# Two accumulating banks in the first channel layer, and nine of twelve second-layer rounds as block products

## The chip, the cores and the metric

The kernel runs on one core of a Trainium2 chip. The metric is the device time of one execution in microseconds (us), the median of several runs; lower is better. The engines are TensorE (PE in the profile; PEld is its weight load), VectorE (DVE), ScalarE (ACT), GpSimd (POOL) and SyncE (SP), which only issues DMAs. All arithmetic that matters here is fp32, and each fp32 matmul in the code shows as two MATMUL instructions in the trace.

## The reference

Attention with a block mask, then a Fourier mixing block with a two-layer channel network:

```python
batch, n_heads, seq, head_dim = (4, 8, 768, 64)
scores = np.where(mask, scale * q @ k.T, -1e9)      # mask: neighbours, first/last and sampled blocks
attn = softmax(scores); x = attn @ v                # bridged to (4, 768, 512)
mixed = np.real(np.fft.fft(np.fft.fft(x, axis=1), axis=2))
u = x + mixed
un = (u - mean(u)) / np.sqrt(var(u) + 1e-06)
ch = np.maximum(un @ w_ch1, 0.0) @ w_ch2            # 512 -> 2048 -> 512
return u + ch
```

## The kernel before, in words

Python code lays out one static instruction stream for each engine, in program order (`manual_schedule`). A small planner keeps a clock for each engine (`when`, advanced by `busy(engine, us, after)`), and decides by it what is issued where.

*Attention* goes in 96 slots (`slot`), 24 a batch. A slot makes two score tiles (L578) in the two PSUM banks of the pool `ps_s`, exponentiates them on ScalarE (in batches 2 and 3 in place, L606), multiplies them by the mask on VectorE (L608), adds the results up on POOL (L638), and multiplies by the values two slots later (L652). Once channel work exists, slots go in pairs: the even one of a pair does all value products that are due, the odd one may do channel work after its scores.

*Mixing* of a batch (`fourier`) is a list of steps, `apart`, that `gap()` inserts between other work where the planner's clocks allow: scaling and folds on VectorE (kind "d"), then products along the sequence (`along`, L856) and across the channels (`across`, L887 to L904), whitening (L951), transposes (`un_flip`, L992, with a copy L993), and operand sums (`right`, L1029). The steps from the first transpose on may start only when at most six entries of channel work are left.

*Channel work* of batches 0 to 2 is the list `late`: four rounds of eight entries, two quads of the first layer and six plain steps of the second. `quad(p)` (L1054) makes two 128-row blocks of the hidden layer for all 768 tokens as two halves, with seven block products in place of eight (the Strassen-Winograd scheme). Its seven products (L1075, 128x384, two matmuls each) are: one into the middle bank `xp`, copied by ScalarE (L1095); one into the middle bank `yp`, used twice; and four into the score banks `z5` and `z7`, each started anew. VectorE adds them up in seven sums (L1080), and ScalarE applies the ReLU in place (L1084). VectorE also forms the operand sums of the next quad (`combine`, `left`, L1042 to L1049). The second layer of a round, `channels` (L1230), is six plain steps of four 512-wide matmuls (L1240) and one VectorE sum (L1243), or, where `seven[r]` is set, three calls of `round_of` (L1171): for a block of tokens in each half seven block products of two 256-wide matmuls (L1183), ScalarE copies (L1188), VectorE sums (L1192, L1222, L1168), and POOL sums (L1152, L1165, L1196). `seven[r]` is set at L1062, only for work done alone, and not for a batch's last round.

How much channel work goes between the attention slots is set at L1606 to L1616: a pace a slot from the planned time left less `COVER`, and `rest()` (L1488), which lets a step go when half of its planned time is owed. The rest is done alone by `until` (L1462) at slot 4 of the next batch but one, when the room of the old batch is needed; the next batch's mixing steps are inserted there. The last batch is done alone at the end, with its own version of the second layer (`outputs`), and is not touched by the change but for its first layer.

Of the kernel before, what the change touches and what calls it, by code (L numbers as in the profile page):

```python
# [99 lines left out]
def kernel(  # L100
# [460 lines left out]
    def scores(us):  # L561

        n, w = divmod(us[0], UP)
# [409 lines left out]
    z_at = [0.0, 0.0]  # L973
    rstd_at = deque()
# [3 lines left out]
    def mixer(b, xA, xB):  # L978
# [75 lines left out]
        def quad(p):  # L1054
# [5 lines left out]
            if not last:  # L1060
                if p % 2 == 0:
                    seven[p // 2] = state["alone"] and p // 2 < NF // 4 - 1  # L1062
                elif seven[p // 2]:
                    state["drain"]()
                    sums_room()
                    for j in (1, 2, 4, 3):
                        round_right(p // 2, j)
# [5 lines left out]
            def product(to, a, c, after=0.0):  # L1073
                for k in range(ND // 2):
                    nc.tensor.matmul(to, a[:, k, :], c[:, k, :], start=(k == 0),  # L1075
                                     stop=(k == ND // 2 - 1))
                return busy("PE", PRODUCT, after) + HOP

            def plus(to, ps, a, at):
                tt(out=to, in0=ps, in1=a, op=ALU.add)  # L1080
                return busy("DVE", SUM, at) + HOP

            def relu(h, at):
                nc.scalar.activation(out=h, in_=h, func=ACT.Relu)  # L1084
                busy("ACT", RELU, at)

            def combine(j):
# [3 lines left out]
            x, at = ps_m.tile([P, 512], FP32, tag="m", name="xp")[:, 0:HS], bank("m")  # L1091
            z5, z7 = (ps_s.tile([P, 2, 512], FP32, tag="s", name=name)[:, 0, 0:HS]
                      for name in ("z5", "z7"))
            done = product(x, a11, b11)
            nc.scalar.copy(out=h11, in_=x)  # L1095
            p1 = busy("ACT", RELU, done) + HOP
            give(at, p1 - HOP)
            y, at = ps_m.tile([P, 512], FP32, tag="m", name="yp")[:, 0:HS], bank("m")
            p2 = product(y, a12, b21)
            done = product(z7, s2, t[2])  # L1100
            u2 = plus(h21, z7, h11, max(done, p1))
            c11 = plus(h11, y, h11, p2)
            relu(h11, c11)
            done = product(z5, s[1], t[1])
            plus(h12, z5, h21, done)
            combine(1)
            done = product(z7, s[3], t[3], u2)
            u3 = plus(h21, z7, h21, done)
            c22 = plus(h22, z5, h21, done)
            z_at[0] = c22  # L1110
            relu(h22, c22)
            combine(3)
            gap(0.0, 1.9)
            done = product(y, a22, t[4], c11)
            c21 = plus(h21, y, h21, done)
            give(at, c21 - HOP)
            relu(h21, c21)
            gap(0.0, 1.9, "t")
            done = product(z7, s[4], b22, u3)
            z_at[1] = plus(h12, z7, h12, done)  # L1120
            relu(h12, z_at[1])
# [10 lines left out]
        def sums_room():  # L1132

            def cut(t, at, k):
                return t[:, at:at + 2 * HS // 3 * k].rearrange("p (k n) -> p k n", k=k)

            rooms = [ep.tile([P, 2 * HS], FP32, tag="e", name="of") for _ in range(4)]
# [7 lines left out]

        def part(r, k, n):
            return w2_sb[:, 4 * r + 2 * k:4 * r + 2 * k + 2, n * DH:n * DH + DH]

        def round_right(r, j):
            a, c = {1: (part(r, 0, 1), part(r, 0, 0)), 2: (part(r, 1, 1), w_t[1]),  # L1150
                    3: (part(r, 1, 1), part(r, 0, 1)), 4: (part(r, 1, 0), w_t[2])}[j]
            nc.gpsimd.tensor_tensor(out=w_t[j], in0=a, in1=c, op=ALU.subtract)  # L1152
            busy("POOL", 1.35)
# [5 lines left out]
        def round_left(m, j):  # L1159
# [4 lines left out]
            if j > 2:  # L1164
                nc.gpsimd.tensor_tensor(out=to, in0=a, in1=c, op=op)  # L1165
                busy("POOL", 0.75, when["DVE"])
            else:
                tt(out=to, in0=a, in1=c, op=op)  # L1168
                busy("DVE", 0.43)

        def round_of(r, m):  # L1171

            after = dict(zip(OUT, OUT[1:])).get(m)
# [4 lines left out]
            u_at, d_at = (ps_s.tile([P, 2, 512], FP32, tag="s", name=name)[:, 0, 0:DH]  # L1178
                          for name in ("yz", "yw"))
# [15 lines left out]
            def later(to, i, at):  # L1195
                nc.gpsimd.tensor_add(out=to, in0=kept[i], in1=to)  # L1196
                busy("POOL", 0.75, at)

            def ahead(*js):
                if after is not None:  # L1200
                    for j in js:
                        round_left(after, j)

            if m == OUT[0]:
                round_left(m, 1)
                round_left(m, 2)
# [3 lines left out]
            k0 = keep(0, u_at, product(u_at, a11, part(r, 0, 0), True, z_at[0]))  # L1210
# [3 lines left out]
            if m == OUT[0]:  # L1214
                round_left(m, 3)
                round_left(m, 4)
            gap(start=0.9)
            k1 = keep(1, u_at, product(u_at, a21, w_t[2], False, k0))
            later(a1, 1, k1)
            k2 = keep(2, d_at, product(d_at, h_s[1], w_t[1], True, z_at[1]))  # L1220
# [3 lines left out]
            z_at[0] = busy("DVE", 0.7, done) + HOP  # L1224
            later(b1, 2, max(z_at[0], k2))
            z_at[1] = plus(a1, d_at, product(d_at, h_s[4], part(r, 1, 1), False, k2))
            ahead(1, 2, 3, 4)
            state["soon"] = 1.6

        def channels(r, half, m):  # L1230

            if seven.get(r):
                round_of(r, m)
                if m == OUT[-1]:
                    for _ in range(T):
                        late.popleft()
                return
# [56 lines left out]
        def outputs(r, m, after):  # L1294
# [27 lines left out]
            ends = r == 1 and after is None  # L1322
            u = sum_p.tile([P, DH], FP32, tag="oT", name="u")
# [457 lines left out]
```

## Time and profile before

| what | value |
|---|---|
| median of three runs | 1064.43 us (1063.6 to 1065.32) |
| the profiled execution, own time | 1066.03 us |
| its span, first to last instruction | 1064.3 us |
| mean granted TensorE clock | 0.987 |
| PE / VectorE / ScalarE / POOL busy | 1026.7 / 708.7 / 382.5 / 328.3 us |
| L1075, first-layer products, PE busy in all | 297.6 us |
| L1240, plain second-layer steps, PE busy in all | 148.8 us |
| L1183, second-layer block products, PE busy in all | 93.4 us |

Lines of a group show: line, engine, operation, output and input tiles, shapes, count, then busy time, mean ns of one, idle time before them and what ended it. Timeline rows show: start, duration, engine, line, operation, tiles, count, and in brackets the idle time before, with what released the engine. Rows of windows show, after the stretch and its width, busy time and count of PE, PEld, DVE, ACT and POOL, then the granted clock, the DMA share and GB/s. Neighbouring matmuls overlap a little in the trace, so a group's sum is best taken from starts.

### The profile page before, as it was taken

How to read it: one execution, taken by the hardware profiler on the slowest of the kernel's cores; microseconds unless marked ns; L12 is line 12 of the kernel's file. 1: busy time of each engine (PE TensorE's matmuls, PEld its weight loads, DVE VectorE, ACT ScalarE, POOL GpSimd, SP SyncE). 2: the span in 40 equal slices, each digit the busy share in tenths (PEclk: the TensorE clock that was granted, in tenths of full speed). 3: DMA queues.
4: the chain of work that ended last, by engine and by line, in shares of the span. 5: the costliest groups of instructions: out<-in, count | busy, mean ns of one | idle time of the engine just before them, and what ended most of it. 6: DMA issues, size and time to landing. Idle time of an engine off the chain costs nothing.

```text
span 1064.3 us, 13217 instructions
## 1 busy us (share of the span) xinstructions
PE 1026.7 (96%) x4594; PEld 572.3 (54%) x4594; DVE 708.7 (67%) x1287; ACT 382.5 (36%) x781; POOL 328.3 (31%) x365
## 2 busy tenths in 40 slices
PE   8999999999999998899999999799999999999996
PEld 4333345445766853444444764353445764578575
DVE  6898795877776566754668476765447736675663
ACT  6978765563222214342430223333221221210210
POOL 1000183556733404545561222645440401000000
PEclk9999999999999999999999999999999999899998
DMA  7857422220000002212120001311000002000001
GB/s 211 229 170 225 107 46 45 45 46 15 1 1 1 1 20 69 38 38 32 35 54 0 1 1 39 67 28 24 8 15 1 1 1 57 3 1 1 1 17 47
DMA packets 120549, 46.32 MB, mean 44 GB/s; under 512 B 108172, under 2 KB 113562, under 8 KB 120474
## 3 DMA queue, kind: packets, MB, share of 16 engines
q1 hardware_dynamic: 119222, 44.66, 17.6%
q10 hardware_dynamic: 1220, 0.72, 0.3%
q8 instruction: 38, 0.62, 0.2%
q14 instruction: 37, 0.30, 0.1%
q0 software_dynamic: 32, 0.01, 0.0%
HBM read 36.72 MB, written 6.29 MB: 40 GB/s over the span
## 4 chain that ended last, share of the span: by engine, by line
PE 84%; DVE 5%; ACT 4%; POOL 2%; issue 2%; DMA 1%; SPq 1%; ACTq 0%; DVEq 0%; POOLq 0%
PE z L1075 15%; PE y L1240 13%; PE s L578 12%; PE o L652 10%; PE yp L1075 7%; PE yy L1308 7%; PE xp L1075 4%; PE yz L1183 3%; PE yw L1183 2%; PE yc L1183 2%; PE zp L856 2%; PE s L588 1%; POOL acc L638 1%; ACT e L598 1%; PE sp L719 1%
## 5 line engine op out<-in xcount | busy, mean ns | idle before, releaser
L638 POOL TENSOR_TENSOR acc<-acc,e 128x384 f32<-128x384 f32 x158 | 162.6, 1062 | 97.0 <-DVE e L608 77.9
L578 PE MATMUL s<-qT,kT 64*128 64x384 f32 x768 | 155.3, 519 | 7.6 <-ACT e L598 5.2
L652 PE MATMUL o<-e,vr 128*64 128x384 f32 x768 | 146.1, 508 | 5.0 <-DVE oT L660 5.0
L638 POOL TENSOR_TENSOR acc<-e 128x384 f32<-128x384 f32 x46 | 49.0, 1084 | 202.4 <-ACT e L598 126.0
L578 PEld LDWEIGHTS s<-qT,kT 64*128 64x128 f32 x768 | 64.7, 188 | 86.5 <-ACT e L598 23.1
L608 DVE TENSOR_TENSOR e<-s,mask 128x768 f32<-128x768 f32 x88 | 79.9, 948 | 46.2 <-ACT s L606 35.6
L606 ACT ACTIVATE s<-s 128x768 f32<-128x768 f32 x88 | 66.8, 791 | 106.1 <-PE s L578 105.7
L598 ACT ACTIVATE e<-s 128x768 f32<-128x768 f32 x104 | 79.0, 809 | 49.0 <-PE s L588 36.5
L1075 PE MATMUL z<-unT,t 128*128 128x384 f32 x256 | 93.4, 488 | 1.6 <-DVE hA L1080 1.6
L652 PEld LDWEIGHTS o<-e,vr 128*64 128x64 f32 x768 | 48.5, 139 | 77.0 <-issue 67.5
L1080 DVE TENSOR_TENSOR hA<-z,hA 128x384 f32<-128x384 f32 x64 | 35.6, 557 | 70.0 <-PE z L1075 70.0
L1084 ACT ACTIVATE hA<-hA 128x384 f32<-128x384 f32 x64 | 33.5, 523 | 123.7 <-DVE hA L1080 123.7
L1240 PE MATMUL y<-w_sb,hA 128*128 128x512 f32 x168 | 74.8, 595 | 0.0
L1240 PE MATMUL y<-w_sb,hB 128*128 128x512 f32 x168 | 74.5, 595 | 0.0
L1196 POOL TENSOR_TENSOR x<-of,x 128x256 f32<-128x256 f32 x45 | 34.9, 783 | 123.2 <-ACT of L1188 83.4
L1075 PEld LDWEIGHTS z<-unT,t 128*128 128x128 f32 x256 | 48.3, 190 | 36.9 <-DVE hA L1080 4.0
L1243 DVE TENSOR_TENSOR x<-y,x 128x512 f32<-128x512 f32 x42 | 29.0, 691 | 57.3 <-PE y L1240 57.3
L1084 ACT ACTIVATE hB<-hB 128x384 f32<-128x384 f32 x64 | 33.5, 523 | 87.2 <-DVE hB L1080 87.2
L1240 PEld LDWEIGHTS y<-w_sb,hB 128*128 128x128 f32 x168 | 31.2, 190 | 38.2 <-issue 38.2
L1240 PEld LDWEIGHTS y<-w_sb,hA 128*128 128x128 f32 x168 | 31.1, 190 | 37.5 <-issue 36.7
L1075 PE MATMUL xp<-unT,w_sb 128*128 128x384 f32 x128 | 49.0, 506 | 0.0
L1075 PE MATMUL z<-t,w_sb 128*128 128x384 f32 x128 | 46.6, 487 | 0.2 <-DVE e L608 0.2
(235 smaller groups left out, 1728.5 us busy)
## 6 DMA issues: line engine op xcount, KB each, us to landing
wraw<-in_moe_w_ch_dram SPq DMA_DIRECT2D x32, 512.0 KB
vr<-in_v_dram SPq DMA_DIRECT2D x30, 192.0 KB
qb<-in_q_dram SPq DMA_DIRECT2D x44, 96.0 KB
kb<-in_k_dram SPq DMA_DIRECT2D x44, 96.0 KB
x<-oT SPq DMA_DIRECT2D x192, 12.0 KB
out_dram<-x SPq DMA_DIRECT2D x11, 252.0 KB
out_dram<-x SPq DMA_DIRECT2D x18, 128.0 KB
qr<-in_q_dram SPq DMA_DIRECT2D x24, 64.0 KB
```

Source lines behind the costliest of these rows:

```text
L578: nc.tensor.matmul(s[:, i, 0:HS], kT[rows, c * P:(c + 1) * P], qT[rows, queries], start=True, stop=u not in by_pe)
L598: nc.scalar.activation(out=e, in_=s[:, :, 0:HS], func=ACT.Exp, scale=scale)
L606: nc.scalar.activation(out=s[:, :, 0:HS], in_=s[:, :, 0:HS], func=ACT.Exp, scale=scale)
L608: nc.vector.tensor_tensor(out=e, in0=s[:, :, 0:HS], in1=m.broadcast_to([P, 2, HS]), op=ALU.mult)
L638: nc.gpsimd.tensor_add(out=acc[:, i, :], in0=start[:, i, :], in1=e[:, i, :])
L652: nc.tensor.matmul(o[D * i:D * i + D, :], vt[:, i, c, :], e[:, i, :], start=(c == 0), stop=(c == C - 1))
L1075: nc.tensor.matmul(to, a[:, k, :], c[:, k, :], start=(k == 0), stop=(k == ND // 2 - 1))
L1080: tt(out=to, in0=ps, in1=a, op=ALU.add)
L1084: nc.scalar.activation(out=h, in_=h, func=ACT.Relu)
L1183: nc.tensor.matmul(to, a[:, k, :], c[:, k, :], start=start and k == 0, stop=k == 1, skip_group_check=True)
L1240: nc.tensor.matmul(y, hs[0, half][:, l, m * P:(m + 1) * P], w2_sb[:, 4 * r + l, :], start=(l == 0), stop=(l == 3))
L1308: nc.tensor.matmul(ps, a[:, k, :], c[k // 2][:, k % 2, :] if isinstance(c, list) else c[:, k, :], start=(k == 0), stop=(k == 3))
```

## The change

Four things are changed at once.

In `quad`, the first product goes into a score bank (`za`) and not into a middle bank. Later products are accumulated into the same bank (`start` false), and ScalarE copies the bank's content out between them (`keep`), so that of seven VectorE sums three remain. `zb` is the second score bank. The last ReLU reads the bank directly. `two_tiles` names the two banks in the order in which they were emptied. One of the two inner `gap` calls goes, the other gets 1.4 for 1.9.

`choose` decides at a round's first quad how its second layer is done: "e" in work done alone (with rooms of the pool `ep`, as before), "big" between attention slots if no mixing step is pending (with two rooms of `big`, and all operand sums on VectorE), and plain for the last round of a batch. It replaces six plain entries in `late` by three blocks, planned at 6.1 each.

`round_of` takes its two score banks through `two_tiles`, and in a round's first token block starts with a product into a score bank.

`COVER` is 117 for 100, and `rest()` lets nothing go between slots while more than 6 and at most 24 entries are left, that is rounds 1 to 3 of a batch. `begin` first finishes an open "big" round.

```diff
+    def two_tiles(name):
+        pair = [ps_s.tile([P, 2, 512], FP32, tag="s", name=name + str(i))[:, 0, :]
+                for i in range(2)]
+        return state["first"], pair[::-1] if state["first"] else pair
...
                 if p % 2 == 0:
-                    seven[p // 2] = state["alone"] and p // 2 < NF // 4 - 1
+                    choose(p // 2)
                 elif seven[p // 2]:
-                    state["drain"]()
-                    sums_room()
+                    sums_room(seven[p // 2])
...
-            def product(to, a, c, after=0.0):
+            def product(to, a, c, start, after=0.0):
                 for k in range(ND // 2):
-                    nc.tensor.matmul(to, a[:, k, :], c[:, k, :], start=(k == 0),
-                                     stop=(k == ND // 2 - 1))
+                    nc.tensor.matmul(to, a[:, k, :], c[:, k, :], start=start and k == 0,
+                                     stop=k == ND // 2 - 1, skip_group_check=True)
                 return busy("PE", PRODUCT, after) + HOP
...
+            i, pair = two_tiles("z")
+            za, zb = (t[:, 0:HS] for t in pair)
+            state["first"] = 1 - i
+            k1 = keep(h11, za, product(za, a11, b11, True, z_at[i]))
             y, at = ps_m.tile([P, 512], FP32, tag="m", name="yp")[:, 0:HS], bank("m")
-            p2 = product(y, a12, b21)
-            done = product(z7, s2, t[2])
-            u2 = plus(h21, z7, h11, max(done, p1))
-            c11 = plus(h11, y, h11, p2)
+            c11 = plus(h11, y, max(k1, product(y, a12, b21, True)))
+            give(at, c11 - HOP)
+            k2 = keep(h12, za, product(za, s2, t[2], False, k1))
+            k4 = keep(h22, zb, product(zb, s[1], t[1], True, z_at[1 - i]))
             relu(h11, c11)
-            done = product(z5, s[1], t[1])
-            plus(h12, z5, h21, done)
             combine(1)
-            done = product(z7, s[3], t[3], u2)
-            u3 = plus(h21, z7, h21, done)
-            c22 = plus(h22, z5, h21, done)
-            z_at[0] = c22
+            gap(0.0, 1.4)
+            done = product(za, s[3], t[3], False, k2)
+            c22 = plus(h22, za, max(done, k4))
+            z_at[1 - i] = plus(h12, zb, product(zb, s[4], b22, False, k4))
             relu(h22, c22)
             combine(3)
-            gap(0.0, 1.9)
-            done = product(y, a22, t[4], c11)
-            c21 = plus(h21, y, h21, done)
-            give(at, c21 - HOP)
-            relu(h21, c21)
-            gap(0.0, 1.9, "t")
-            done = product(z7, s[4], b22, u3)
-            z_at[1] = plus(h12, z7, h12, done)
-            relu(h12, z_at[1])
+            done = product(za, a22, t[4], False, c22)
+            relu(h12, z_at[1 - i])
+            z_at[i] = relu(h21, done, za)
             combine(4)
...
+        def choose(r):
+
+            seven[r] = None
+            if r < NF // 4 - 1 and late:
+                seven[r] = "e" if state["alone"] else None if apart else "big"
+            if seven[r]:
+                quad_next = late.popleft()
+                for _ in range(2 * T):
+                    late.popleft()
+                late.extendleft((lambda m=m: round_of(r, m), 6.1) for m in OUT[::-1])
+                late.appendleft(quad_next)
+                state["open"] = T + 1 if seven[r] == "big" else 0
...
+        def aside(r, out, a, c, op, n, at=0.0, sooner=False):
+
+            if seven[r] == "big" or sooner:
+                tt(out=out, in0=a, in1=c, op=op)
+                return busy("DVE", n * 0.0011 + 0.15, at) + HOP
+            nc.gpsimd.tensor_tensor(out=out, in0=a, in1=c, op=op)
+            return busy("POOL", n * 0.0026 + 0.07, at) + HOP
...
-            u_at, d_at = (ps_s.tile([P, 2, 512], FP32, tag="s", name=name)[:, 0, 0:DH]
-                          for name in ("yz", "yw"))
+            i, pair = two_tiles("yz")
+            u_at, d_at = (t[:, 0:DH] for t in pair)
...
+            def first():
+                k.append(keep(0, u_at, product(u_at, a11, part(r, 0, 0), True, z_at[i])))
 
             if m == OUT[0]:
-                round_left(m, 1)
-                round_left(m, 2)
+                for j in (1, 2):
+                    round_left(r, m, j)
+                first()
             c_at, at = ps_m.tile([P, 512], FP32, tag="m", name="yc")[:, 0:DH], bank("m")
             a_at = plus(a0, c_at, product(c_at, a12, part(r, 1, 0), True))
             give(at, a_at - HOP)
-            k0 = keep(0, u_at, product(u_at, a11, part(r, 0, 0), True, z_at[0]))
+            if m != OUT[0]:
+                first()
...
-    COVER = 100.0
+    COVER = 117.0
+    KEPT = (NF // 4 - 1) * (2 + 2 * T)
...
     def begin(b):
 
+        while state["open"]:
+            channel_step()
+            gap()
...
     def rest():
 
-        return state["owed"] if late and state["owed"] >= late[0][1] / 2 else 0.0
+        if not late or 2 * T < len(late) <= KEPT or state["owed"] < late[0][1] / 2:
+            return 0.0
+        return state["owed"]
```

## The prediction

> **What bounds the kernel now.** I read the busy table first, then the windows of 25 us, then the timeline of TensorE in three places. The busy table:
>
> ```profile
> PE 1026.7 (96%) x4594; PEld 572.3 (54%) x4594; DVE 708.7 (67%) x1287; ACT 382.5 (36%) x781; POOL 328.3 (31%) x365
> ```
>
> TensorE is the bound: 1064.3 − 1026.7 = 37.6 us of it are idle. So two things count: matmul time, and waits of TensorE. VectorE's 67% counts only where TensorE waits for it. The chain of waits agrees: 84% of the span is PE. The windows say where the idle time lies:
>
> ```profile
> 400.00:425.00 25.00, 22.32 (x93) 10.12 (x93) 16.66 (x24) 10.99 (x20) 12.66 (x16) 0.95 0.31 74
> 425.00:450.00 25.00, 22.20 (x91) 10.24 (x87) 19.39 (x25) 9.56 (x21) 15.16 (x14) 0.91 0.24 37
> 500.00:525.00 25.00, 25.00 (x101) 11.72 (x99) 11.93 (x19) 8.43 (x18) 6.92 (x8) 1.00 0.19 37
> 675.00:700.00 25.00, 21.95 (x96) 10.43 (x97) 18.71 (x23) 10.73 (x22) 15.55 (x15) 0.93 0.24 51
> 900.00:925.00 25.00, 21.97 (x74) 13.36 (x73) 18.17 (x39) 7.09 (x13) 3.31 (x7) 0.86 0.08 21
> ```
>
> The first number after the width is PE busy, the third from the end the granted clock. PE loses time, and clock, three times, where a batch's channel work runs out and the next batch's Fourier mixing isn't ready: I call these the three seams (around 400-440, 650-690, 900-908). Between the seams, as at 500-525, PE is full. The timeline of TensorE, at the seams, in attention, and in the rounds:
>
> ```profile
> 421.16 0.66 PE L992 MATMUL utp<-ident,un 128*128 128x128 f32 x4 [1.94 <-DVE un L951]
> ...
> 436.25 2.83 PE L652 MATMUL o<-e,vr 128*64 128x384 f32 x8 [2.51 <-DVE oT L660]
> ...
> 454.25 1.56 PE L578 MATMUL s<-qT,kT 64*128 64x384 f32 x8
> ...
> 456.11 1.82 DVE L608 TENSOR_TENSOR e<-s,mask 128x768 f32<-128x768 f32 x2 [1.16 <-ACT s L606]
> 456.53 1.56 PE L1075 MATMUL xp<-unT,w_sb 128*128 128x384 f32 x4
> ...
> 459.21 1.45 PE L1075 MATMUL z<-t,w_sb 128*128 128x384 f32 x4
> ...
> 524.57 1.72 PE L578 MATMUL s<-qT,kT 64*128 64x384 f32 x8
> 527.58 1.78 PE L578 MATMUL s<-qT,kT 64*128 64x384 f32 x8 [1.29 <-DVE e L608]
> ...
> 565.26 10.46 PE L1240 MATMUL y<-w_sb,hB 128*128 128x512 f32 x24
> 575.57 1.45 PE L1075 MATMUL xp<-unT,w_sb 128*128 128x384 f32 x4
> ...
> 597.87 1.03 PE L1183 MATMUL yc<-w_sb,hA 128*128 128x256 f32 x4
> 598.73 1.03 PE L1183 MATMUL yz<-w_sb,hA 128*128 128x256 f32 x4
> ```
>
> **A, products of the second layer: −10.3 us.** A plain round starts at 554.86 and the next quad at 575.57: 20.71 us. A block product starts 0.864 us after the one before (597.87, 598.73), and a round has 21: 18.14. Batch 0 already has three such rounds, batches 1 and 2 one each (L1183: 60 matmuls a group, 12 a round, so five). Nine means four more: 4 × 2.57 = 10.3. Their operand sums lie on POOL when channel work is alone (there PE waited for POOL 0.6 us in all five rounds), and on VectorE in the two rounds between attention slots, where VectorE is idle half of the time (11.9 of 25 us at 500-525): nothing. The added ScalarE copies (three of 0.37 a block) go to an engine 36% busy: nothing.
>
> **B, first layer: its first product moves into a score bank: +10.1 us.** Seven products of 1.29 us stay. Four of seven VectorE sums (0.56 each) go, two ScalarE copies (0.48) come. In a quad alone, a copy starts 0.09 us after its product and has one product (1.29) between itself and the next write to its bank, so half a microsecond is left: nothing, unless a ScalarE Fourier copy (0.37 to 0.59) stands ahead. In attention it's otherwise. Channel work follows the scores of every second slot. Today `xp` and `yp` have banks of their own: 2.6 us pass before the first `z` needs a score bank (456.53 to 459.21). Now product one wants it at once. Scores at 454.25 leave PE free 1.49 us later; the first mask product (half of the 456.11 row) ends at 457.06, 2.8 us after the scores: a wait of some 1.35. Four quads stay in these slots: 5.4. A round's first token block starts in a score bank too (1.35); the other two have one product of 0.86 ahead, so 0.5 each: 2 × 2.35 = 4.7. Behind the waiting product stand the rest of the quad and the next scores on TensorE, for which the exponentials on ScalarE and POOL's sums wait in turn. Ends: 5 (transposes or sums of other work fall in between) and 13.
>
> **C, slots left without channel work: +3.6 us.** Two scores in a row without work between wait 1.29 (527.58). The new `rest()` lets one round in (quads planned at 9.1, blocks 6.1, the last 24 entries kept back). Pace is max(2.5, (155.6 − 117)/16) = 2.5 a slot, capped at 5.0; a quad goes at 4.55 owed, a block at 3.05. Worked slot by slot, with steps in odd slots only, the nine odd slots from 439 to 548 get work in five; now it is seven. So two more bare slots a phase: one with row sums in it (0.85 us of PE, so 0.5), one of 1.3; two phases. The quads moved out of the slots issue no DMA, so SyncE's queue stays as it is. Ends: 1 and 8 (POOL's 7.7 us of sums per two slots becoming the limit).
>
> **D, scores behind a quad: +2.3 us.** The bank the next scores take first is now emptied last, by the ReLU from the bank after product seven: 0.1 + 0.52 + semaphores, some 0.85 after PE could start. Four quads, a third of them with value products in between. Ends 0 and 4.
>
> **E, the gap inside a quad: +3 us.** Product seven now writes the bank that VectorE's `c22` sum reads, with 0.4 us to spare. Ahead of that sum the code puts a combine, which can't start before product four has read its operand (5.4 us into the quad; the planner's clock has it done at 3.8), and then Fourier steps until 1.4 us past the planned PE time. A step of 1.8 us then makes product seven wait 0.5. Behind it on VectorE wait `c22`, the `h12` sum, the ReLUs, and so the next quad's first bank. About two quads a seam have such steps pending: 6 × 0.5. Ends 0 and 9. The trace of before has no such wait; the nearest row is product seven's 0.20 at 254.75.
>
> **F, the seams: −13 us.** Idle there: 5.5 (0.73, 1.94, 0.29, 2.51), 5.7 and 3.0. Slow rows behind them: the value products at 436.25 took 2.83 for a usual 1.51, those at 688.70 the same, the first product at 907.93 took 2.76 for 1.45, three transposes before it 1.1 for 0.65: 5.3 together. In all 19.5. Their cause is that the mixing chain is late: its last frequency block runs at 643.30 and 890.95, after the last plain round began (639.87, 876.09), and only then the transposes and whitening start. Three things bring the chain forward: VectorE is relieved of 4 × 0.56 us a quad, one middle bank is free earlier (`xp` is gone), and round 1's quads move into the part that covers it (95.7 us of channel work alone become 111). That is some 15 us, against a lateness of 10 to 24. I take two thirds; the one transpose bank and the mask products stay in the way. Ends 0 and −19.5.
>
> **Sum:** −10.3 + 10.1 + 3.6 + 2.3 + 3 − 13 = −4.3. The profiled execution took 1066.0 (span 1064.3), 1.6 above the median of 1064.4 of the runs; a difference carries over to the median: 1060. About 0.2% (2 us) is what a measurement here can tell from no change.
>
> **A rule against it.** Row first: after the wait of 1.29 at 527.58 the next eight took 1.78, against 1.56 after none, and the clock in 525-550 was 1.00; after 2.51 the next took 1.3 us more and the window's clock was 0.91. The Trainium skill, page "TensorE: Matmul & The Clock Gate", section "A second HAM failure mode: psum-queue depth-cycling", says that frequent micro-idles between groups of matmuls, from cycling through banks, make the clock fall back between half and full. By that rule B to D would each be paid for again, and the sum would be some 18 us higher.
>
> **Rivals.**
> 1. *The seams stay* (slower). The chain's pace is set by how many gaps it is offered and by one transpose bank, not by VectorE. For it: between its blocks at 610 and 627 VectorE was idle 2.6 us in one stretch, and a quad now offers one inner gap, not two. Against it: the bank that went free. Then F is −1 and the sum +7.7: 1072. It decides from F above −6.
> 2. *Dips behind each short wait.* 14 new waits in B and C, each followed by 1.3 us as behind 436.25: +18 on 1060, 1078. Against it: the row at 527.58.
> 3. *The interleaved rounds aren't done as blocks*, because Fourier steps are still pending when the round opens, which the code tests. Then A is 5.1 and the rounds' part of B goes: 1060 + 5.2 − 4.7, and the slots no longer end in time, some 3 more: 1064.
> 4. *In balance:* F near −7, the rest as above: 1066.
>
> **Chances.** Forecast 0.50 (1050 to 1062; the top is what counts as faster); in balance 0.09 and rival 3 0.03, both within 0.2%; rival 1 0.31 (1067 to 1076); rival 2 0.07. Faster 0.50, same 0.12, slower 0.38. The range: below, F at its end and B to D at their low ends would give 1046, and I cut at 1050; above, it takes in rival 1 to 1074. The likeliest one's own range is 1050 to 1062.
>
> **What would show it.** PE busy falls by some 10 us. L1183's groups have 108 matmuls each, plain channels 72 for each half. In attention of batches 2 and 3, waits of the first-layer products for the mask product (L608) appear, about 1.35 each, 20 times at most with the bare slots; the next scores wait for a ScalarE ReLU. At the three seams waits of L992's transposes for the whitening shrink or go, and so do the clock's 0.91, 0.93 and 0.86. In quads alone only product seven waits, for VectorE. The prediction is wrong if the seams keep their 14 us idle, if waits in attention are under 5 us or over 25, or if the copies on ScalarE hold up product three.

## The result, and the profile after

The changed kernel takes 1076.45 us (median of six runs, 1073.83 to 1079.92); beside it the kernel before took 1065.07 (six runs). The ratio is 1.0112, with a 95% interval of 1.0089 to 1.0135: slower by 11.4 us. The forecast was 1060 with a range of 1050 to 1074, so it was wrong, and on the wrong side.

The profiled execution took 1073.83 us, with a span of 1072.1. That is the fastest of the six (2.6 us under the median), and the one of before was 1.0 above the median of the six runs beside the change, so the two traces show 7.8 us of the 11.4. Line numbers from here on are those of the changed kernel: L579 scores, L609 mask products, L653 value products, L804 VectorE's folds, L1080 first-layer products, L1089 their VectorE sums, L1165 POOL's sums, L1205 block products. The busy table of the changed kernel:

```profile
PE 1015.3 (95%) x4738; PEld 597.3 (56%) x4738; DVE 686.0 (64%) x1245; ACT 424.4 (40%) x881; POOL 365.0 (34%) x403
```

TensorE's busy time fell by 11.4 us (from 1026.7), about what the products were to save; that the two agree is partly luck, since the clock took part too (below). Its idle time rose from 37.6 to 1072.1 − 1015.3 = 56.8, by 19.2. The loss is in waits. The windows (busy time of PE first after the width, third from the end the granted clock) say where:

```profile
400.00:425.00 25.00, 22.61 (x87) 10.48 (x88) 19.44 (x22) 9.23 (x16) 11.26 (x10) 1.00 0.21 48
425.00:450.00 25.00, 23.61 (x103) 11.50 (x103) 16.57 (x19) 13.00 (x27) 14.84 (x14) 1.00 0.24 53
500.00:525.00 25.00, 21.26 (x112) 10.52 (x108) 15.76 (x21) 10.85 (x18) 16.80 (x18) 1.00 0.34 61
675.00:700.00 25.00, 18.78 (x91) 8.41 (x90) 19.32 (x23) 10.93 (x22) 17.07 (x18) 0.93 0.25 57
725.00:750.00 25.00, 20.54 (x89) 9.72 (x89) 16.02 (x22) 10.04 (x16) 10.28 (x10) 0.96 0.10 22
900.00:925.00 25.00, 23.53 (x79) 12.45 (x78) 13.37 (x29) 5.48 (x11) 2.86 (x6) 1.00 0.24 61
```

The first and third seam got better: the clock is 1.00 where it was 0.95, 0.91 and 0.86. The second got no better. New holes are in attention, which was full before: 3.7 us idle at 500-525, 4.5 at 725-750. TensorE's waits, by what it waited for (us in all, times, longest):

```profile
PE s L579 <- DVE e L609: 8.6, 8, 2.2
PE z L1080 <- DVE hB L1089: 7.1, 4, 2.2
PE yz L1205 <- DVE e L609: 5.2, 5, 3.2
PE z L1080 <- DVE e L609: 4.5, 5, 1.3
PE utp L998 <- DVE un L952: 1.9, 1, 1.9
```

The next scores wait for the mask product for 8.6 us (2.1 before). Product seven waits 7.1 us for VectorE's `c22` sum; before, products waited for first-layer sums 1.6 us in all. First products of quads and blocks wait 4.5 + 5.2 us for the mask product. The transposes' wait for the whitening fell from 5.5 to 1.9.

Two places show how the waits come about. First, a quad in work done alone, with VectorE's folds (L804), POOL's operand sums of the next round (L1165) and TensorE's products:

```profile
577.43 1.98 POOL L1165 TENSOR_TENSOR wt<-w_sb 128x512 f32<-128x512 f32 x1
578.20 1.49 DVE L804 SCALAR_TENSOR_TENSOR e<-sa,not_first,e 128x257 f32<-128x257 f32 x1
579.49 1.33 POOL L1165 TENSOR_TENSOR of<-w_sb,wt 128x512 f32<-128x512 f32 x1
579.61 1.49 DVE L804 SCALAR_TENSOR_TENSOR sa<-sa,not_first 128x257 f32<-128x257 f32 x1
580.90 1.33 POOL L1165 TENSOR_TENSOR of<-w_sb,of 128x512 f32<-128x512 f32 x1
581.02 1.49 DVE L804 SCALAR_TENSOR_TENSOR sa<-sa,ident 128x257 f32<-128x257 f32 x1
...
586.23 1.01 DVE L1089 TENSOR_TENSOR hB<-z,hB 128x384 f32<-128x384 f32 x2
...
586.83 2.33 PE L1080 MATMUL z<-t,w_sb 128*128 128x384 f32 x4 [2.18 <-DVE hB L1089]
...
587.83 0.48 DVE L804 SCALAR_TENSOR_TENSOR sd<-sd,not_first 128x257 f32<-128x257 f32 x1
...
588.96 2.42 PE L1080 MATMUL z<-unT,w_sb 128*128 128x384 f32 x4
```

A fold takes 1.49 us while POOL adds, and 0.48 once POOL is done (587.83). The three folds of 1.49 end 0.28 us behind the end of the POOL sum that was running when they began (577.43 + 1.98 = 579.41, and 578.20 + 1.49 = 579.69, in the first pair). So VectorE comes to `c22` late, product seven waits 2.18, and then it and the next product take 2.33 and 2.42 for a usual 1.56 (behind a wait) and 1.45; the granted clock from 586.8 to 590.3 is 0.60. Second, the first block of a round between attention slots:

```profile
746.76 0.58 DVE L661 STREAM_TRANSPOSE oT<-o 128x384 f32<-128x384 f32 x1 [3.15 <-DMA x<-oT]
747.27 1.78 DVE L609 TENSOR_TENSOR e<-s,mask 128x768 f32<-128x768 f32 x2
748.24 2.07 PE L1205 MATMUL yz<-w_sb,hA 128*128 128x256 f32 x4 [3.17 <-DVE e L609]
750.11 1.63 PE L1205 MATMUL yc<-w_sb,hA 128*128 128x256 f32 x4
```

VectorE's transpose waits 3.15 us until a DMA has read the last user of its buffer. The mask products stand behind it, and the block's first product needs the score bank that they read. A plain step, which starts in a middle bank, would have run there.

### The profile page after: what moved, and what is told of

Same layout as the page of the kernel before. It is cut to its first block, busy times and chain, and to the rows that moved or that the text cites. A ratio compares the mean times of both kernels' runs of the same rounds, so it can differ in the third digit from the quotient of the medians.

```text
span 1072.1 us, 13705 instructions
## 1 busy us (share of the span) xinstructions
PE 1015.3 (95%) x4738; PEld 597.3 (56%) x4738; DVE 686.0 (64%) x1245; ACT 424.4 (40%) x881; POOL 365.0 (34%) x403
## 4 chain that ended last, share of the span: by engine, by line
PE 75%; DVE 12%; ACT 4%; SPq 3%; issue 3%; DMA 2%; POOL 0%; DVEq 0%; ACTq 0%; POOLq 0%
PE z L1080 21%; PE yz L1205 10%; PE s L579 8%; PE o L653 8%; PE yy L1330 7%; PE y L1262 6%; PE yc L1205 4%; PE yp L1080 3%; SPq L692 3%; DVE e L609 2%; PE zp L857 2%; ACT s L607 1%; PE s L589 1%; DVE t L1035 1%; ACT e L599 1%
## 5 line engine op out<-in xcount | busy, mean ns | idle before, releaser
L579 PE MATMUL s<-qT,kT 64*128 64x384 f32 x768 | 154.9, 517 | 13.7 <-DVE e L609 8.6
L653 PE MATMUL o<-e,vr 128*64 128x384 f32 x768 | 143.1, 500 | 4.3 <-DVE oT L661 2.5
L579 PEld LDWEIGHTS s<-qT,kT 64*128 64x128 f32 x768 | 64.0, 186 | 92.3 <-DVE e L609 27.8
L609 DVE TENSOR_TENSOR e<-s,mask 128x768 f32<-128x768 f32 x88 | 80.1, 949 | 44.6 <-ACT s L607 44.5
L1080 PE MATMUL z<-t,w_sb 128*128 128x384 f32 x256 | 94.7, 493 | 8.5 <-DVE hB L1089 7.1
L1165 POOL TENSOR_TENSOR x<-of,x 128x256 f32<-128x256 f32 x63 | 45.6, 730 | 137.1 <-DVE x L1214 82.6
L653 PEld LDWEIGHTS o<-e,vr 128*64 128x64 f32 x768 | 47.8, 136 | 72.9 <-issue 64.6
L1080 PE MATMUL z<-unT,t 128*128 128x384 f32 x256 | 87.8, 486 | 0.0
L1080 PEld LDWEIGHTS z<-t,w_sb 128*128 128x128 f32 x256 | 48.0, 190 | 45.7 <-DVE hB L1089 12.6
L1210 ACT COPY of<-yz 128x256 f32<-128x256 f32 x81 | 30.2, 373 | 98.8 <-PE yz L1205 97.8
L1085 ACT COPY hB<-z 128x384 f32<-128x384 f32 x64 | 30.7, 479 | 94.1 <-PE z L1080 94.1
L1080 PEld LDWEIGHTS z<-unT,t 128*128 128x128 f32 x256 | 47.9, 190 | 31.3
L1089 DVE TENSOR_TENSOR hB<-z,hB 128x384 f32<-128x384 f32 x64 | 35.1, 554 | 35.8 <-PE z L1080 35.6
L1055 DVE TENSOR_TENSOR t<-w_sb 128x256 f32<-128x256 f32 x88 | 35.9, 439 | 33.1 <-PE z L1080 33.1
L1080 PE MATMUL z<-unT,w_sb 128*128 128x384 f32 x128 | 49.0, 506 | 4.8 <-DVE e L609 4.5
L1249 DVE TENSOR_TENSOR x<-x,yz 128x512 f32<-128x512 f32 x27 | 18.5, 687 | 46.0 <-PE yz L1205 46.0
L940 POOL TENSOR_SCALAR st<-st 128x1 f32<-128x1 f32 x24 | 8.2, 343 | 114.4 <-DVE st L939 113.9
```

The source lines that it names most:

```text
L579: nc.tensor.matmul(s[:, i, 0:HS], kT[rows, c * P:(c + 1) * P], qT[rows, queries], start=True, stop=u not in by_pe)
L609: nc.vector.tensor_tensor(out=e, in0=s[:, :, 0:HS], in1=m.broadcast_to([P, 2, HS]), op=ALU.mult)
L653: nc.tensor.matmul(o[D * i:D * i + D, :], vt[:, i, c, :], e[:, i, :], start=(c == 0), stop=(c == C - 1))
L1055: tt(out=s[j], in0=a, in1=c, op=op)
L1080: nc.tensor.matmul(to, a[:, k, :], c[:, k, :], start=start and k == 0, stop=k == ND // 2 - 1, skip_group_check=True)
L1165: nc.gpsimd.tensor_tensor(out=out, in0=a, in1=c, op=op)
```

## The experiments

Times are medians; differences between versions are made from the ratios to the kernel before that ran beside each (before: 1064.1 to 1065.8 us).

| version | block rounds, in slots | us | ratio, 95% interval |
|---|---|---|---|
| changed kernel | 9, 2 | 1076.45 | 1.0112 [1.0089, 1.0135] |
| layer1_only | 5, 0 | 1063.09 | 0.9985 [0.9972, 0.9997] |
| layer2_only | 9, 2 | 1082.8 | 1.0179 [1.0159, 1.0199] |
| slots_old_order | 9, 2 | 1079.76 | 1.0151 [1.0133, 1.0168] |
| gap_after_c22 | 9, 2 | 1066.37 | 1.0022 [1.0006, 1.0039] |
| no_big | 7, 0 | 1064.71 | 1.0000 [0.9986, 1.0014] |
| no_big_gap_late | 7, 0 | 1060.19 | 0.9961 [0.9944, 0.9978] |
| layer1_gap_late | 5, 0 | 1064.73 | 1.0005 [0.9991, 1.0019] |
| sums_on_vector | 9, 2 | 1067.43 | 1.0027 [1.0016, 1.0038] |
| five_rounds_vector | 5, 0 | 1059.87 | 0.9959 [0.9942, 0.9976] |
| seven_rounds_vector | 7, 0 | 1054.5 | 0.9906 [0.9887, 0.9925] |
| seven_rounds_vector_gap_late | 7, 0 | 1057.82 | 0.9939 [0.9922, 0.9956] |
| slot_blocks_middle_first | 9, 2 | 1065.69 | 1.0016 [1.0007, 1.0026] |
| plain_in_pairs | 7, 0 | 1061.5 | 0.9966 [0.9953, 0.9979] |
| slot_blocks_fewer_sums | 9, 2 | 1065.37 | 1.0008 [0.9996, 1.0020] |

### Which half of the change loses

In the first four expectations, theory 1 puts the loss on the new first layer and its waits for VectorE, theory 2 on the nine rounds and the slots that they empty.

The new first layer alone:

```diff
-                seven[r] = "e" if state["alone"] else None if apart else "big"
+                seven[r] = "e" if state["alone"] else None
...
-    COVER = 117.0
+    COVER = 100.0
...
-        if not late or 2 * T < len(late) <= KEPT or state["owed"] < late[0][1] / 2:
+        if not late or state["owed"] < late[0][1] / 2:
```

> Only the first layer is changed; the second layer and the pace between slots are as before (five rounds as blocks, COVER 100, no entries kept back). Theory 1 (the time is lost in waits of TensorE that the first layer's new banks bring: first products on the mask product in attention, product seven on VectorE): eight quads lie between slots instead of four, so 8 x 1.3 = 10 us of waits of L1080 for the mask product, 3 to 6 us of waits for L1089, none of the 10.3 us gain; 1072 to 1080 us. Theory 2 (the loss lies in the second layer: VectorE and POOL slow each other in the added rounds): 1056 to 1066 us.

It measured 1063.1, a little faster than before. With the same products as before, TensorE is busy for 5.1 us less (1021.6), mostly because the clock no longer falls in the first and third seam (1.00 in their windows). A fall of the clock at 295 us, behind a wait of 1.89 for the `c22` sum, is new. First products wait for the mask product 7.4 us, and what the seams gain pays for it. So the first layer by itself isn't the loss.

The nine rounds with the old first layer (`quad` as before, everything else as changed):

> Only the second layer and the pace are changed (nine rounds as blocks, 24 entries kept back); the quads are as before. Theory 1: products -10, block products still wait for the mask product 5 us, bare slots 6.5 us of scores on the mask product, seams as before: 1064 to 1069 us. Theory 2: as the changed kernel, 1073 to 1079 us.

1082.8, slower still than both together and above both ranges; theory 2's is the nearer one. Its seams are worse than before's (transposes wait 6.9 us for the whitening and 6.3 for the sums ahead of it).

The old order of products in the slots alone (quads there as before, and blocks with a middle bank first):

> The changed kernel, but between attention slots a quad has the old form (first two products in middle banks) and a round's blocks start with their two products in middle banks. Theory 1: the 9.7 us of first products waiting for the mask product go: 1064 to 1068 us. Theory 2: 1073 us or more.

1079.8: no gain. The waits of first products went, and others came: 4.2 us for `z7` sums (2.1 at 452.08), 2.0 for ScalarE's copies, 1.6 for operand sums; the next scores' wait for the mask product stayed (8.7 in all, from 8.6). TensorE is idle for 57.2 us, against 56.8. The wait that B priced is real, but it isn't the price of the order.

The Fourier steps inside a quad after the `c22` sum:

```diff
             combine(1)
-            gap(0.0, 1.4)
...
             combine(3)
+            gap(0.0, 1.4)
             done = product(za, a22, t[4], False, c22)
```

> The changed kernel with the inner gap of a quad moved behind the sums c22 and h12, so that no Fourier step stands ahead of them on VectorE. Theory 1: product seven's 7.1 us of waits for VectorE go and nothing takes their place: 1067 to 1071 us. Theory 2: the steps delay something else, 1074 us or more.

1066.4: 9.6 us faster than the changed kernel, 0.6 us below theory 1's range. Product seven's waits fell only from 7.1 to 4.4 us, so most of it is not that wait: the steps land at other places, and in this trace the scores' wait for the mask product fell too (8.6 to 6.2) and the blocks' as well (5.2 to 3.0). Why these fell isn't shown.

### The rounds between slots, and the place of the gap

Theory 3 from here on: TensorE work taken out of the slots becomes waits there. Theory 4: the order of VectorE's work in the parts done alone is the loss. `no_big` has the first line of `layer1_only`'s diff alone, `no_big_gap_late` that and the gap, `layer1_gap_late` the gap in `layer1_only`.

> The changed kernel, but no round is done as blocks between attention slots: seven block rounds, all in work done alone, and six plain steps in the slots of each phase again; the rest as in the changed kernel (1076.5). Theory 3 (the slots): TensorE work taken out of the odd slots, and tied to a score bank, turns into waits for the mask product; with plain steps there the two phases get back some 6 to 10 us and lose 2 x 2.57 of TensorE time: 1069 to 1073. Theory 4 (the order of VectorE's work in the parts done alone, where the Fourier steps stand ahead of the c22 sum): the slots are not the loss, and the kernel pays the 5 us of products: 1077 to 1082.

1064.7: 11.9 us faster than the changed kernel, though it has two block rounds (5.1 us) fewer. Theory 3 has the sign, and its size was too small. The two rounds between slots are over half of the matter.

> As before, and the Fourier steps inside a quad stand behind the c22 sum. Theory 3: the gap's place saves only the waits of product seven, about half of what it saved with nine rounds: 1063 to 1068. Theory 4: the same 10 us as with nine rounds, from a higher level: 1067 to 1072. If both hold, 1058 to 1062, the fastest so far.

1060.2, 4.2 us faster still: in the range where both hold. The saving is about half of the 9.6, as theory 3 had it.

> The new first layer alone (1063.1), with the Fourier steps inside a quad behind the c22 sum. Theory 3: product seven waited only 1.9 us there, so 1061 to 1064. Theory 4: the place of the gap is worth some 10 us whatever the second layer does: 1052 to 1057.

1064.7, about 2 us slower than with the early gap. The gap's place has no worth of its own here; it helped only with the added block rounds, which points to something else that makes VectorE late. That was the question for the next run.

### POOL beside VectorE

```diff
-            nc.gpsimd.tensor_tensor(out=out, in0=a, in1=c, op=op)
+            tt(out=out, in0=a, in1=c, op=op)
             return busy("POOL", n * 0.0026 + 0.07, at) + HOP
```

> The changed kernel (1076.5), same order of instructions on TensorE, but POOL's operand sums and additions of the rounds done alone are given to VectorE, with the planner's clocks left as they were. Theory 5 (POOL's sums beside VectorE's stretch VectorE's folds, 0.48 to 1.49 us each, and so hold the mixing chain and seam 2 open): folds back at 0.48, the chain ends some 10 us earlier, 1066 to 1071. Theories 3 and 4: VectorE gets about 50 us more work just where it is queued: no gain, 1075 to 1085.

1067.4: VectorE got 133 instructions more and the kernel 9 us faster. The same folds and the same product seven, in the trace of this run:

```profile
575.99 0.48 DVE L804 SCALAR_TENSOR_TENSOR e<-sa,not_first,e 128x257 f32<-128x257 f32 x1
...
576.38 0.48 DVE L804 SCALAR_TENSOR_TENSOR sa<-sa,not_first 128x257 f32<-128x257 f32 x1
576.78 0.48 DVE L804 SCALAR_TENSOR_TENSOR sa<-sa,ident 128x257 f32<-128x257 f32 x1
...
581.80 1.20 DVE L1089 TENSOR_TENSOR hB<-z,hB 128x384 f32<-128x384 f32 x2
...
582.41 1.56 PE L1080 MATMUL z<-t,w_sb 128*128 128x384 f32 x4
...
583.80 1.45 PE L1080 MATMUL z<-unT,w_sb 128*128 128x384 f32 x4
```

The folds are at 0.48, the quad runs through, and product seven's waits are 0.6 us in all instead of 7.1. VectorE's busy time grew by only 29 us (686.0 to 715.1) for the 120 us that POOL lost (365.0 to 244.9). The two traces differ by 5.2 of the 9 us, as the one of the changed kernel was its fastest execution and this one was 1.2 above its median. The expectation named the second seam. The first slot quad behind it starts 5.2 us earlier (693.6 against 698.8), but the seam's own idle time (650 to 700) hardly changed, 6.9 to 6.7 us: this was won in the quads ahead of it, as in the rows shown. So theory 5 has the cause right and the place wrong.

The Trainium skill, page "SBUF — State Buffer", section "SBUF: two separate sides", says that VectorE and GpSimd share one pair of ports, and that a VectorE instruction with two operands in SBUF and a GpSimd instruction that reads SBUF lock each other out for a whole instruction. The trace of the changed kernel agrees: a fold with two operands in SBUF that begins inside a POOL sum ends 0.28 us behind it, and the POOL sum at 577.43, which began inside a VectorE sum of 1.10 us, took 1.98 for 1.27. VectorE's sums with one operand in PSUM did not grow: 48 of L1214 ran at least half beside a POOL sum and took 0.39 to 0.43 us, the 33 others 0.41 to 0.43.

The trace of the kernel before had such rows already, the last two folds of the same mixing, where one runs beside POOL:

```profile
585.60 0.48 DVE L803 SCALAR_TENSOR_TENSOR sd<-sd,not_first 128x257 f32<-128x257 f32 x1
585.65 1.56 POOL L1152 TENSOR_TENSOR of<-w_sb 128x512 f32<-128x512 f32 x1 [22.32 <-PE o L652]
586.12 1.37 DVE L803 SCALAR_TENSOR_TENSOR sd<-sd 128x257 f32<-128x257 f32 x1
```

The second of these folds takes 0.43 us alone (588.34 in the changed kernel).

### Best of both

> The new first layer alone (1063.1: five rounds, cover and kept-back entries as in the kernel before), with POOL's operand sums on VectorE. Theory 5: only 1.9 us of such waits were left there: 1060 to 1063, so that the two further rounds done alone are worth 4 to 5 us. If keeping entries back (C) is a loss by itself: 1055 to 1058, no slower than seven rounds.

1059.9, 2.8 us under `layer1_only` and 0.1 below theory 5's range. What the same edit is worth in the kernel before, with its old first layer, was not run.

> Seven block rounds, none between slots (1064.7), with POOL's operand sums of the rounds done alone on VectorE. Theory 5 (POOL beside VectorE's folds makes product seven wait): the 7.1 us of waits for the c22 sum fall to about 0.6, as they did with nine rounds: 1056 to 1059. Rival (the 9 us came of the attention slots, that is of other timing behind the seam): 1061 to 1066.

1054.5: 1% faster than the kernel before (ratio 0.9906 [0.9887, 0.9925]), below both ranges, and the fastest version. Between five rounds and seven lie 5.6 us, where 2 × 2.57 were worked out. Done alone, without POOL in the way, a block round earns its products, and the kept-back entries cost nothing that shows. The sum of waits of product seven is 0.6 us here too.

> The same with the Fourier steps inside a quad behind the c22 sum. Theory 5: both edits take away the same wait of product seven, so no more than 2 us on top of either: 1055 to 1059. If they act on different waits: 1050 to 1054.

1057.8, 3.5 us slower than with the early gap. By these totals, the gap's place and POOL act on largely the same loss, and with POOL out of the way the late gap only does harm.

### Why a round in slots doesn't pay

`sums_on_vector` and `seven_rounds_vector` differ only in the two rounds between slots: 12.9 us for the worse, with 5.1 us of products saved, so 18 us of waits and slowed matmuls (in the traces TensorE's idle time grows by 11.6 us). In starts on TensorE from the second slot quad of a phase to the first quad behind the slots:

| us | batch 2's phase | batch 3's phase |
|---|---|---|
| seven_rounds_vector | 87.8 | 58.9 |
| plain_in_pairs | 93.6 | 60.3 |
| sums_on_vector (blocks) | 92.2 | 66.5 |
| slot_blocks_middle_first | 93.1 | 62.9 |
| slot_blocks_fewer_sums | 92.1 | 63.3 |

Blocks begun in middle banks:

```diff
+            if seven[r] == "big":
+                second()
+            if not early:
                 first()
```

> Nine rounds with POOL's operand sums on VectorE (1067.4), the same order of quads, blocks and slots; only the six blocks between attention slots begin with their two products into middle banks, so that the first product into a score bank comes 1.7 us later. Theory 3b (a block waits because its first product needs a score bank, and the slow rows behind that wait come with it): of the 12.9 us that the two rounds in slots cost, the waits 1.31 + 3.16 + 4 x 0.25 and some 3 us of slow rows go: 1060 to 1063. Theory 3c (three blocks fill three odd slots where six plain steps filled six, so the bare slots wait, and VectorE's operand sums stand ahead of the mask products; the waits move to the next scores): 1065 to 1069.

1065.7, 1.2 us faster: theory 3c. First products wait 0.7 us instead of 5.2, but 3.6 us of new waits stand in the same blocks (for ScalarE's copies 2.0, for operand sums 1.6), and the next scores wait 8.7, from 8.0.

Two plain steps at a time, in the very slots that the blocks have:

```diff
+            if r < NF // 4 - 1 and late and not state["alone"] and not apart:
+                quad_next = late.popleft()
+                six = [late.popleft() for _ in range(2 * T)]
+                late.extendleft((lambda a=six[i][0], c=six[i + 1][0]: (a(), c()), 6.1)
+                                for i in (4, 2, 0))
+                late.appendleft(quad_next)
```

> The fastest version so far (seven_rounds_vector, 1054.5), with the plain steps of the round between attention slots done two at a time: the slots that hold channel work are then the same as with nine rounds (1067.4), three of a round's odd slots and not six, but with plain steps in a middle bank and no operand sums on VectorE. Theory 3c (the emptied odd slots wait): some 1.3 us for each of three to four bare slots in two phases, less what the value products hide: 1058 to 1062. Theory 3d (the block itself is what waits: its score bank, its sums in VectorE's queue): 1053.5 to 1056.5.

1061.5: 6.4 us slower than the same steps one at a time, with the same products and no block between slots. TensorE in this version, in slots where nothing is left to do, with one row of VectorE:

```profile
513.91 1.78 PE L579 MATMUL s<-qT,kT 64*128 64x384 f32 x8 [1.30 <-DVE e L609]
515.61 2.80 PE L653 MATMUL o<-e,vr 128*64 128x384 f32 x16
...
522.60 0.58 DVE L661 STREAM_TRANSPOSE oT<-o 128x384 f32<-128x384 f32 x1 [4.15 <-DMA kb<-in_k_dram]
...
524.08 2.93 PE L579 MATMUL s<-qT,kT 64*128 64x384 f32 x8 [3.39 <-DVE e L609]
526.94 4.38 PE L653 MATMUL o<-e,vr 128*64 128x384 f32 x16
```

The same wait in the list of waits, first of `plain_in_pairs`, then of `seven_rounds_vector`:

```profile
PE s L579 <- DVE e L609: 9.8, 8, 3.4
```

The second, without the emptied slots:

```profile
PE s L579 <- DVE e L609: 3.8, 5, 1.7
```

The emptied slots cost 6.0 us of waits and, behind the wait of 3.39, rows of 2.93 and 4.38 us for a usual 1.56 and 2.80. That covers the loss of batch 2's phase: 93.6 against 92.2 with blocks. VectorE isn't late here for work of its own: it is idle for 4.15 us, until its transpose at 522.60 no longer has to wait for a DMA, and the mask product stands behind the transpose. The code writes each half's `oT` out by 16 small DMAs, which SyncE issues one after the other (from 508.68 to 518.90 here), and with less TensorE work between them the slots catch up with these DMAs. In `seven_rounds_vector` no such transpose waits for a DMA; in the changed kernel two do, 2.96 us at 522.01 and 3.15 at 746.76. No version with these DMAs arranged otherwise was run, so how much of the 18 us they are stays open.

In batch 3's phase, 60.3 against 66.5, it is the first block that meets such a transpose, 3.16 us and slow rows behind it, as at 748.24 above.

> Nine rounds with POOL's sums on VectorE (1067.4), same order on TensorE, but in the two rounds between attention slots 34 of VectorE's operations are left out: the operand sums of the second and third token block (16) and the additions of the kept copies (18). The output lacks these sums; the time alone is read. Theory 3e (these sums, some 0.43 us each and up to 1.2 beside POOL, stand ahead of the mask products in VectorE's queue): of the 18 us that the slots lose, bare slots take 7 and the bank 2, and the sums most of the other 9: 1058 to 1062. Theory 3f (VectorE has room for them; the rest is the clock and the wait for the transpose that waits for its DMA): 1065 to 1068.

1065.4: 2.0 us faster, nearer to theory 3f. Batch 3's phase is 3.2 us shorter without 34 of VectorE's operations, batch 2's no shorter. So of the 18 us, 6.4 are emptied slots. By the table, 8.8 more lie in batch 3's phase (66.5 − 60.3, and the 2.6 of products that a block round saves), and 1.2 in batch 2's (92.2 − 93.6 + 2.6). Of the 8.8, 6.3 are the wait of 3.16 and the four rows behind it (2.08, 1.91, 1.91 and 1.37 us for 1.03 each). Taken away one at a time, VectorE's sums give back 2.0 and the bank's order 1.2. The last 1.6 us stay open; in the profiled run of `sums_on_vector` the second seam (675 to 700), where this edit changes nothing, had a clock of 0.89. Whether POOL could do the operand sums in the slots stays open too: a version that gave them to POOL (`slot_sums_on_pool`, expected at 1067 to 1072 if these sums hold up the mask products, at 1075 to 1085 if not) had engines that wait for each other in a circle, and gave no time.

## Why the prediction was wrong, step by step

**A, the products: right in itself, wrong in "nothing".** The counts came as said (108 matmuls a group of blocks), and a round done alone earns what was worked out (5.6 us for two, from 5.1). But "Their operand sums lie on POOL ... nothing" failed. I looked for TensorE's waits for POOL, which were 0.6 us, and not for what POOL does to VectorE beside it. The trace of before had a fold of 1.37 beside a POOL sum. With two more rounds done alone, POOL's weight sums fall beside four folds on end; all of POOL's block sums together cost 9 us in the changed kernel, against 2.8 with the old five rounds and the new first layer. This is the first failed step. VectorE's share, the sums in the slots, was also put at nothing; leaving 34 of them out gave 2.0 us.

**B, the first product:** 4.5 + 5.2 = 9.7 us of waits of first products, forecast 10.1. The size was right, in part by luck: 3.17 of it is the one wait at 748.24 behind a DMA. The meaning wasn't right: with the old order as much waiting stood elsewhere (`slots_old_order`). That fits a bound by the cycle of scores, exponential, mask product and bank, where the order of products only says who shows the wait.

**C, slots without work:** 3.6 forecast; the scores' wait for the mask product grew by 6.5 us (5.1 without the first seam's window, 400 to 450), and `plain_in_pairs` puts emptied slots alone at 6.4, with slow rows behind the longest. This is the second failed step: I priced two more bare slots a phase at 0.5 and 1.3, and took SyncE's queue to stay as it is. It does, but the emptied slots catch up with it: transposes that wait 2.96 and 3.15 us for DMAs hold back the mask products, and with them the scores at 523.50 (2.20) and the block at 748.24 (3.17). A and C together mean that block rounds in slots, forecast at B's 4.7 and C's 3.6 for 5.1 saved, cost 12.9 net.

**D, scores behind a quad:** nothing. The scores at 453.27 and 708.04 follow their quad without a wait.

**E, the inner gap:** 7.1 us for 3, inside its ends (0 to 9). The mechanism was named rightly (Fourier steps ahead of the `c22` sum) and its size was not: the forecast had a step of 1.8 us ahead of the sum, about four folds at 0.48, and these four took 5.7 us (578.20 to 583.92).

**F, the seams:** in the windows, idle time at the seams fell by 1.7 and 1.6 us in the first and third and rose by 1.2 in the second. But the windows of the first two now also hold a first product's wait of 1.31 each (444.05 and 698.82), which is B's; without them idle time fell by 4.7 us. By the granted clock, 6.4 us of slow matmuls went (busy time times what the clock lacked, 7.7 before, 1.3 after; the prediction had counted 5.3 and left out the rows of 2.29 and 3.72 us behind the wait at 421.16). Together −11.1 for −13, so this step held in the sum, though only two seams gained. Why the second stayed isn't shown. The folds there end 54 us after the work alone begins, against 34 before; but in `sums_on_vector` and `layer1_only`, where they take 0.48 us again, the idle time there is 6.7 and 6.9 us all the same.

By these rows the sum is −10.3 + 9.7 + 5.1 + 0 + 5.5 (7.1 less the 1.6 that product waits for first-layer sums were before) − 11.1 = −1.1, where the spans show +7.8. So 8.9 us lie in rows for which the forecast's sum had no term. Two falls of the clock behind new waits, at 587 and 748 us, make 3.3 (products of 2.33, 2.42, 2.07 and 1.63 us for 1.56, 1.45, 1.13 and 1.03). Two other waits grew: for `oT` at 534.67 by 1.8, and for `peak` at 762.96 by 1.6. Against them, a fall of the clock at 70 us, 1.4 us in the trace of before, didn't come. The other 3.6 us are not taken apart.

The experiments, which go by medians, lead to the same two steps: POOL's sums cost 9 us where E had 3, and block rounds in slots 12.9 where B and C had 3.2 net of the products. On a forecast of 1060 that is 1075.7, beside 1076.5 measured. That it closes so well is luck in part: D's 2.3 that didn't come and F's 1.9 that fell short nearly cancel.

**The rivals.** Rival 1 had a price near the result (1072) and the wrong mechanism: two of three seams shrank, and the clock stayed up in them. Rival 2, dips behind short waits, came only in small part: 3.3 us of its 18, half of it behind a wait of E. In this trace the dips stand behind waits of 2.18 us and more, and not behind the 1.3 us ones that it counted. Rival 3 didn't come: the interleaved rounds were done as blocks.

## What to carry to other kernels

When work moves onto an engine that seems to have room, look at the mean duration of its neighbours' instructions in the new company, not only at who waits for it: here POOL's sums cost nothing by the waits of before and 9 us by VectorE's folds. In a stage paced by a chain through several engines (scores, exponential, mask, bank), saved TensorE time bought nothing here; fewer, larger portions of filler left its slots bare, and small portions in a bank of their own filled them best. Take a change apart by its places before giving it up: done only where TensorE is the bound, and with the sums off POOL, this one is 1% faster instead of 1% slower.

## What the runs showed of the hardware

- A fold of 0.48 us with two operands in SBUF took 1.49 with POOL's sums (1.33 each) beside it, in three rows on end; VectorE's 48 sums of L1214 that read one operand from PSUM beside a POOL sum stayed at 0.39 to 0.43. When VectorE did POOL's 120 us of sums itself, its busy time grew by 29 us.
- A wait of about 2 us may or may not slow what follows. The same wait of 2.18 us for the `c22` sum was followed by products of 2.33 and 2.42 us in the changed kernel and of 1.56 and 1.45 in `no_big`; one of 1.89 was followed by 2.18 and 2.56 in `layer1_only`. The shortest single one was 1.66 us at 411.60 in `slot_blocks_fewer_sums` (rows of 1.96 and 5.17 for a usual 1.78 and 3.70), the longest that slowed nothing was 3.27 us at 532.31 in `layer1_gap_late` (1.56 and 1.45). Shorter waits close together can do it too: 0.68, 0.68 and 1.21 us between 900 and 905 in the kernel before, with transposes of 1.12 for 0.65 behind them. After single waits of 1.3 us the next row was longer by 0.2 us at most; after 3.16 and 3.39 it took 2.08 for 1.03 and 2.93 for 1.56. The Trainium skill, page "TensorE: Matmul & The Clock Gate", section "What's actually happening", puts the fall of the clock at an idle window of about 3.4 us that runs free of the kernel. The chance that the same wait meets agrees with a window that runs free; that 1.66, 1.89 and 2.18 us are enough does not agree with its length.
